# Strided attention pairs in three blocks of residue classes instead of eight, on one core

## The chip, the cores and the metric

The kernel runs on one core of a Trainium2 chip. The metric is the device time in microseconds (us) of one execution; the median of three runs stands for the kernel.

## The reference, cut to what matters

The first part is attention over 8 batches, 8 heads, 576 tokens and a head size of 64. Heads 0 to 3 see a local window; heads 4 to 7 see only earlier tokens of the same residue modulo 32 (the strided heads). The second part is a two-layer network with a squared ReLU on all 4608 tokens.

```python
scores = q @ k.T / 8
mask_local   = (rel >= 0) & (rel < 32)              # rel = query - key; heads 0-3
mask_strided = (rel >= 0) & (key % 32 == query % 32) # heads 4-7
attn = softmax(where(mask, scores, -1e9))
x = (attn @ v)        # tokens x 512, all heads side by side
y = relu(x @ w_in) ** 2 @ w_out                      # 512 -> 2048 -> 512
```

## The kernel before, in words

Work on attention goes by units. A unit is one batch and a pair of heads, numbered u = 4 * batch + pair; pairs 0 and 1 of a batch are local, pairs 2 and 3 strided. The network goes by nine chunks of 512 tokens: `mm1(c, i)` makes one 128-row block of the hidden layer, `mm2(c, i)` a quarter of an output tile. Both run on TensorE (PE) between the attention steps.

A unit goes through these steps. `step_S` multiplies keys with queries into PSUM, and ScalarE (ACT) takes the exponential into a tile `e`. VectorE (DVE) multiplies with a mask (the function `masks`). `step_D` multiplies `e` with V, to which a column of ones is added, so that the sum of each row comes out too; DVE takes the reciprocal of that sum (`rinv`) and multiplies (`x_l` or `x_s`). `step_E` transposes the result into `xt`, the input of `mm1`.

For a strided pair the 576 tokens are sorted by residue modulo 8, because tokens of different residue never meet: eight blocks of 72 tokens for each head. So `step_S` has 16 small matmuls for a pair, `step_D` has 16 in three parts (6, 6 and 4), each part with its own reciprocal and product, and `step_E` has eight PE transposes. Batches 0 and 1 have versions of their own (`step_N`, `step_O`), which the change leaves.

The loads matter here. For a strided pair, q and k are cast to bf16 from DRAM into a DRAM scratch tile by a DMA that GpSimd (POOL) issues (`cast_str_dram`, `q_d` and `k_d`, L165). A transposing DMA issued by SyncE (SP) then brings them into SBUF (`transpose_str`, `qT_s` and `kT_s`, L173). V of batches 2 to 4 is cast straight into its tile `vs` by POOL's DMAs (`load_v_str_direct`, L617). V of batches 5 to 7 comes as fp32 by SP's DMAs into `v_st` (L245), and POOL casts it (L252). Local q and k of batches 5 to 7 are loaded by SP (L114), cast by POOL (L140) and transposed by SP's DMAs (L201).

The order is the program's own. Each engine and each queue runs its instructions in the order in which they were written down, and hooks tie loads and steps to the places between the matmul groups. PE's attention steps are spread over the groups by weights. Three places tie the queues together.

- `load_v_local_gated(b)`, L605: before POOL issues batch b's local V (`vl`), it copies one element of the transposed k of the same batch, so it waits until that has landed. It is used for batches 2 and 3.
- `hold_sync(4)`, L609: SP issues a tiny DMA that reads the last row of batch 4's last V tile, so that SP goes on only when that V has landed. Batch 4's transposes and all of batch 5's loads stand behind it.
- POOL's order for the batches 2 to 5 is: rows (local q and k), casts of q and k, gate, local V, strided V, then rows and casts of the next batch. Casts of batch 5 follow batch 4's V.

In batches 6 and 7 the result of a strided pair is written to DRAM (`x_d`, L446) and transposed back by a DMA (L447); in batches 2 to 5, PE transposes it.

Of the kernel before, what the change touches and what calls it, by code (L numbers as in the profile page):

```python
# [14 lines left out]
def kernel(  # L15
# [21 lines left out]
    NBS = 2 * NJ  # L37
    VP = 72

    singles = ctx.enter_context(tc.tile_pool(name="singles", bufs=1))  # L40
# [32 lines left out]
    mask_full = singles.tile([128, NL, QL], BF16)  # L73
    mask_str = singles.tile([SP_, 1, SP_], BF16)
    vl_all = singles.tile([128, NV, 2, NL, VP], BF16, name="vl")
    vls = [vl_all[:, i] for i in range(NV)]
    vss = [singles.tile([SP_, NBS, VP], BF16, name=f"vs{i}") for i in range(NV)]
    vl_sts = [singles.tile([128, 2 * NL, D], FP32, name=f"vl_st{i}") for i in range(2)]
# [83 lines left out]
    def cast_str_dram(b):  # L162
        for name, src in (("q", q), ("k", k)):
            t = dram.tile([4 * SP_, NJ * D], BF16, name=f"{name}_d")
            nc.gpsimd.dma_start(  # L165
                out=t.rearrange("(x y) c -> x (y c)", x=16),
                in_=src[b, H // 2:H].rearrange("h (x y) d -> (h x) (y d)", x=4))
            big[b, name] = t

    def transpose_str(b):  # L170
        for name in "qk":
            o = strT.tile([128, NJ // 2, 4 * SP_], BF16, name=f"{name}T_s")
            nc.sync.dma_start_transpose(out=o, in_=big.pop((b, name)))  # L173
            came[b] = o[0:1, 0, 0:1]
            for i in range(2):
                st.setdefault(4 * b + 2 + i, {})[name + "T"] = o[:, :, 2 * SP_ * i:2 * SP_ * (i + 1)]

# [47 lines left out]

    def load_v_str_sw(b):
        t = v_st.tile([SP_, 2, NJ * D], FP32, name="v_st")
        t = t.rearrange("p h c -> p (h c)").bitcast(BF16).rearrange("p (h c) -> p h c", h=4)
        nc.gpsimd.dma_start(out=t, in_=v[b, 4:8].rearrange("h (p j) d -> p h (j d)", j=NJ))
        for i in range(2):  # L230
            st.setdefault(4 * b + 2 + i, {})["vf"] = t[:, 2 * i:2 * i + 2]

    def load_v_local_sw(b):
# [5 lines left out]
        for u in range(2):  # L239
            st.setdefault(4 * b + u, {})["v"] = vls[i + u]  # L240

    def load_v_str(u, eng):
        b, p = units[u]
        t = v_st.tile([SP_, 2, NJ * D], FP32, name="v_st")
        eng.dma_start(out=t, in_=v[b, 2 * p:2 * p + 2]  # L245
                      .rearrange("h (p j) d -> p h (j d)", j=NJ))
        st.setdefault(u, {})["vf"] = t

    def cast_v_str(u, copy=None):
        s = st[u]  # L250
        t = vss[v_slot(u)]
        (copy or nc.gpsimd.tensor_copy)(t[:, :, 0:D], s["vf"].rearrange("p h (j d) -> p (h j) d", d=D))  # L252
        s["v"] = t
# [55 lines left out]
    def step_S(u, at_once=False):  # L309
        s = st[u]  # L310
        qT, kT = s["qT"], s["kT"]
        local = is_local(u)
        w, n = (QL, NL) if local else (SP_, NJ)
        kn = 128 if local else SP_
        hn = n // 2
        e = es[u % 4]
        s["e"] = e
        pss = [[None, None], [None, None]]
        for half in range(2):
            for row in range(2):  # L320
                pss[row][half] = bank("pt")
                if u < 4:
                    bias = bias_l[:, half].rearrange("p t c -> p (t c)") if local \
                        else bias_s.rearrange("p t c -> p (t c)")
                    nc.tensor.matmul(pss[row][half][0:kn, 0:S // 2], ident[0:kn, 0:kn], bias,
                                     start=True, stop=False, skip_group_check=True)
            for i in range(hn):
                t = half * hn + i
                klo = w * t
                for row in range(2):  # L330
                    rows = slice(64 * row, 64 * row + 64)
                    if not local:
                        c0 = w * (t // 4)
                        lhsT, rhs = (a[rows, t % 4, c0:c0 + w] for a in (kT, qT))
                    else:
                        lhsT, rhs = kT[rows, klo:klo + kn], qT[rows, w * t:w * (t + 1)]
                    nc.tensor.matmul(pss[row][half][0:kn, w * i:w * (i + 1)], lhsT, rhs,  # L337
                                     start=u > 3, stop=True, skip_group_check=u < 4)
# [11 lines left out]
        def masks(row):  # L350
            x = e[0:kn, S * row:S * (row + 1)].rearrange("p (t c) -> p t c", c=w)
            m = mask_full if local else mask_str.to_broadcast([kn, n, w])
            nc.vector.tensor_tensor(x, x, m, op=ALU.mult)  # L353
# [51 lines left out]
    def step_D(u, part):  # L405
        run_due(lambda x: x[1] == u)
        s = st[u]
        e, vt = s["e"], s["v"]
        if is_local(u):
            w, kn, n0, n1, tot = QL, 128, 6 * part, 6 * part + 6, 2 * NL  # L410
            rhs = vt.rearrange("p h t d -> p (h t) d")
            pos = lambda n: QL * n
            src = lambda n: n
        else:
            w, kn, tot = SP_, SP_, NBS
            n0, n1 = ((0, 6), (6, 12), (12, 16))[part]
            rhs = vt
            pos = lambda n: SP_ * blk_pos(n % 2, n // 2)
            src = lambda n: NJ * (n % 2) + n // 2
        po = bank("ph" if u < 2 else "pt")[:, 0:6 * (D + 1)].rearrange("p (n d) -> p n d", d=D + 1)  # L420
        for n in range(n0, n1):
            nc.tensor.matmul(po[:, n - n0, :], e[0:kn, pos(n):pos(n) + 128],  # L422
                             rhs[0:kn, src(n), 0:D + 1], start=True, stop=True)
        if part == 0:
            s["x"] = (xl_pool if is_local(u) else x_pool).tile(
                [w, tot, D], BF16, name="x_l" if is_local(u) else "x_s")
        x = s["x"]
        if is_local(u):
            x = x.rearrange("p (t h) d -> p h t d", h=2)[:, part]
        else:  # L430
            x = x[:, n0:n1, :]
        m = n1 - n0
        rinv = small.tile([128, 6, 1], FP32, name="rinv")
        nc.vector.reciprocal(rinv[0:w, 0:m], po[0:w, 0:m, D:D + 1])  # L434
        nc.vector.tensor_tensor(x, po[0:w, 0:m, 0:D],  # L435
                                rinv[0:w, 0:m].to_broadcast([w, m, D]), op=ALU.mult)

    def step_E(u):
# [3 lines left out]
        local = is_local(u)  # L442
        n, w = (NL, QL) if local else (NJ, SP_)
        if not local and b >= XD:
            xd = dram.tile([S, 2 * D], BF16, name="x_d")
            nc.sync.dma_start(out=xd.rearrange("(p j) c -> p (j c)", j=NJ), in_=x.rearrange("p n d -> p (n d)"))  # L446
            nc.sync.dma_start_transpose(out=xt[p][:, b * S:(b + 1) * S], in_=xd)  # L447
            st.pop(u)
            return
# [6 lines left out]
        px = bank("pt").bitcast(BF16)[:, 0:S]  # L456
        for t in range(n):
            nc.tensor.transpose(px[:, w * t:w * (t + 1)],  # L458
                                x[:, 2 * t:2 * t + 2, :].rearrange("p h d -> p (h d)"),
                                ident[0:w, 0:w])  # L460
        dst = xt[p][:, b * S:(b + 1) * S]
        copy = nc.scalar.copy if u < 12 else nc.vector.tensor_copy
        if local:
            copy(dst, px)
        else:
            copy(dst.rearrange("c (p j) -> c p j", j=NJ),
                                  px.rearrange("c (j p) -> c p j", j=NJ))
        st.pop(u)
# [100 lines left out]
    def stream_steps(lo, hi, base):  # L569
        order = [T_(lo, "q"), T_(lo, "k"), T_(lo + 1, "q"), S_(lo), T_(lo + 1, "k"), lambda: None]  # L570
        ends = {}
        for u in range(lo, hi + 1):
# [10 lines left out]
            if u < hi:  # L583
                if more:
                    order.append(T_(u + 2, "q"))
                order.append(D_(u, 1))
                if not is_local(u):
                    order.append(D_(u, 2))
        return order, ends
# [18 lines left out]
    def hold_sync(b):  # L608
        nc.sync.dma_start(out=dram.tile([1, 2], BF16, name="hold"),  # L609
                          in_=vss[v_slot(4 * b + 3)][0:1, NBS - 1, 0:2])  # L610

    def load_v_str_direct(b):
        for u in (4 * b + 2, 4 * b + 3):
            t = vss[v_slot(u)]
            h = 2 * units[u][1]
            for i in range(2):
                nc.gpsimd.dma_start(out=t[:, NJ * i:NJ * (i + 1), 0:D],  # L617
                                    in_=v[b, h + i].rearrange("(p j) d -> p j d", j=NJ))
            st.setdefault(u, {})["v"] = t
# [61 lines left out]
    def late_constants():  # L681
# [4 lines left out]
        for t in vss:  # L686
            nc.vector.memset(t[:, :, D:D + 1], 1.0)
        for i, e in enumerate(es):
# [5 lines left out]
    for fn, spare in first:  # L694
        fn()
        warm(spare)
        tick()
    late_constants()
    loads_1()

# [66 lines left out]
    def D_all(u):  # L767
        return [D_(u, i) for i in range(2 if is_local(u) else 3)]

# [14 lines left out]
    second(23, ts("k", 1))  # L784
    second(24, E_(5))
    second(25, S_(6, True))
    second(27, S_(7, True))
# [66 lines left out]
```

## Time and profile before

| | |
|---|---|
| median of 3 runs | 309.14 us (308.31 to 309.71) |
| the profiled execution's own time | 314.03 us |
| its span, first to last instruction | 312.3 us |
| PE busy | 299.8 us (96%) |
| DVE, ACT, POOL busy | 157.9, 167.3, 73.7 us |
| DMA packets, bytes | 94118, 40.75 MB |
| POOL's queue, SP's queue: share of 16 engines | 41.0%, 35.8% |
| mean granted TensorE clock | 0.989 |

A profile is of one execution; this one took 1.6% longer than the median. "L422" is line 422 of the kernel. In the views, PE is the matmuls and PEld their weight loads; SPq and POOLq are the sequencers of these engines. A line of the waits reads: the engine and line that waited, for whom, microseconds in total, times, longest. A line of a timeline reads: start, length, engine, line, operation, output and input, count, and in brackets the idle time before it and who ended it. POOL's time on a DMA line is the time to issue it, not to move the data. The DMA row of the page gives the busy share of the 16 DMA engines in 40 slices of the span, 7.8 us each.

### The profile page before, as it was taken

The page shows a single profiled execution, that of the slowest core. Times are in us where ns is not written, and L with a number is a line of the kernel's source. Part 1 is how long each engine was busy: PE and PEld are TensorE (multiplying, and loading weights), DVE is VectorE, ACT ScalarE, POOL GpSimd, SP SyncE. Part 2 cuts the span into 40 slices and gives each one's busy share as a digit, 9 for nine tenths or more (in the row PEclk, how much of TensorE's full clock was granted, in tenths as well). Part 3 has the DMA queues.
Part 4 walks back from the last instruction along what each step waited for, and adds up shares of the span by engine and source line. Part 5 has one row for each costly group of instructions (what it writes and reads, how often), then busy time and mean ns, then how long its engine had stood idle before and what let it go on. Part 6 is the DMA issues. An engine that isn't in the chain of part 4 may idle for free.

```text
span 312.3 us, 6071 instructions
## 1 busy us (share of the span) xinstructions
PE 299.8 (96%) x2326; PEld 150.9 (48%) x2368; DVE 157.9 (51%) x405; ACT 167.3 (54%) x346; POOL 73.7 (24%) x103
## 2 busy tenths in 40 slices
PE   8799999999999999799999999999999999999995
PEld 3554554544655554344445454444444444444444
DVE  5346764558777865567467668544522222222200
ACT  3666746889567765355545455555443434344311
POOL 8553400630971004434065134000000000000000
PEclk9959999999999999999999999999999999999999
DMA  8999996995999998989899884212221001001121
GB/s 158 177 205 204 191 221 132 177 187 108 154 197 141 100 161 188 198 181 215 141 242 226 213 197 100 73 52 55 71 73 67 35 34 36 34 34 36 48 87 68
DMA packets 94118, 40.75 MB, mean 130 GB/s; under 512 B 78858, under 2 KB 87754, under 8 KB 93898
## 3 DMA queue, kind: packets, MB, share of 16 engines
q0 software_dynamic: 34528, 15.00, 41.0%
q1 hardware_dynamic: 59562, 25.37, 35.8%
q8 instruction: 18, 0.29, 0.4%
q14 instruction: 10, 0.08, 0.1%
HBM read 37.64 MB, written 13.57 MB: 164 GB/s over the span
## 4 chain that ended last, share of the span: by engine, by line
PE 85%; DMA 5%; DVE 4%; POOL 2%; issue 2%; ACT 1%; SPq 0%; POOLq 0%; DVEq 0%
PE ph L482 35%; PE py L522 26%; PE ph L522 9%; PE pt L337 3%; PE pt L422 3%; DMA vl<-in_v_dram 3%; DMA kTl<-k_l 2%; PE pt L482 2%; PE pt L288 1%; PE pt L458 1%; PE ph L504 1%; DMA vl_st<-in_v_dram 1%; PE pt L522 1%; DVE x_l L435 1%; DVE e L353 1%
## 5 line engine op out<-in xcount | busy, mean ns | idle before, releaser
L482 PE MATMUL ph<-xt,w_in_b 128*128 128x512 bf16 x534 | 138.2, 380 | 1.2 <-issue 0.5
L488 ACT ACTIVATE r<-ph 128x512 bf16<-128x512 f32 x138 | 82.3, 597 | 94.1 <-PE ph L482 90.1
L491 DVE TENSOR_TENSOR g_sb<-r 128x512 bf16<-128x512 bf16 x144 | 64.9, 452 | 107.8 <-ACT r L488 106.6
L522 PE MATMUL py<-w_out_b,g_sb 128*128 128x512 bf16 x385 | 100.8, 379 | 0.9 <-issue 0.2
L482 PEld LDWEIGHTS <-w_in_b 128*128 128x128 bf16 x576 | 52.5, 98 | 55.8 <-issue 1.0
L522 PEld LDWEIGHTS <-g_sb 128*128 128x128 bf16 x560 | 50.8, 98 | 54.7 <-issue 0.4
L347 ACT ACTIVATE e<-pt 72x288 bf16<-72x288 f32 (+1 forms) x128 | 45.7, 407 | 12.2 <-PE pt L337 12.2
L522 PE MATMUL ph<-w_out_b,g_sb 128*128 128x512 bf16 x139 | 34.2, 379 | 0.2
L422 PEld LDWEIGHTS <-e 128*128 128x128 bf16 (+1 forms) x384 | 20.5, 98 | 15.9 <-issue 1.7
L435 DVE TENSOR_TENSOR x_s<-pt,rinv 72x384 bf16<-72x384 f32 (+1 forms) x36 | 18.3, 509 | 1.2
L526 ACT COPY y<-py 128x512 f32<-128x512 f32 x25 | 14.6, 585 | 7.0 <-PE py L522 6.3
L353 DVE TENSOR_TENSOR e<-e,mask_str 72x576 bf16<-72x576 bf16 x28 | 14.2, 518 | 3.8 <-ACT e L347 3.7
L435 DVE TENSOR_TENSOR x_l<-pt,rinv 96x384 bf16<-96x384 f32 x28 | 15.5, 554 | 1.0
L434 DVE RECIPROCAL rinv<-pt 96x6 f32<-96x6 f32 (+2 forms) x64 | 11.8, 184 | 6.5 <-PE pt L422 6.3
L353 DVE TENSOR_TENSOR e<-e,mask_full 128x576 bf16<-128x576 bf16 x28 | 12.7, 455 | 1.9 <-ACT e L347 1.7
L220 POOL CAST vl<-vl_st 128x768 bf16<-128x768 f32 x6 | 5.7, 950 | 31.0 <-DMA vl_st<-in_v_dram 30.9
L422 PE MATMUL pt<-vs,e 72*128 72x65 bf16 x192 | 12.1, 194 | 0.7 <-DVE e L353 0.3
L526 ACT COPY y<-ph 128x512 f32<-128x512 f32 x9 | 5.2, 583 | 13.3 <-PE ph L522 13.1
L140 POOL CAST q_l<-q_st 96x768 bf16<-96x768 f32 x6 | 5.2, 866 | 28.0 <-DMA q_st<-in_q_dram 27.9
L617 POOL DMA_DIRECT2D vs<-in_v_dram x12 | 9.7, 817 | 0.0
L422 PE MATMUL pt<-vl,e 128*128 128x65 bf16 x168 | 9.7, 193 | 0.0
L337 PEld LDWEIGHTS <-kT_s 64*72 64x72 bf16 x256 | 6.1, 115 | 7.0 <-issue 6.2
(110 smaller groups left out, 203.6 us busy)
## 6 DMA issues: line engine op xcount, KB each, us to landing
out_dram<-y SPq DMA_DIRECT2D x35, 256.0 KB, 2.3
w_out_b<-in_moe_w_out_dram POOLq DMA_DIRECT2D x4, 512.0 KB, 14.4
q_d<-in_q_dram POOLq DMA_DIRECT2D x6, 288.0 KB, 8.0
k_d<-in_k_dram POOLq DMA_DIRECT2D x6, 288.0 KB, 9.3
q_st<-in_q_dram SPq DMA_DIRECT2D x12, 144.0 KB, 4.1
k_st<-in_k_dram SPq DMA_DIRECT2D x12, 144.0 KB, 4.0
vl_st<-in_v_dram SPq DMA_DIRECT2D x12, 144.0 KB, 3.1
v_st<-in_v_dram SPq DMA_DIRECT2D x6, 288.0 KB
```

The costliest lines, as they stand in the source:

```text
L337: nc.tensor.matmul(pss[row][half][0:kn, w * i:w * (i + 1)], lhsT, rhs, start=u > 3, stop=True, skip_group_check=u < 4)
L347: nc.scalar.activation(e[0:kn, lo:lo + S // 2], pss[row][half][0:kn, 0:S // 2], AF.Exp, scale=scale)
L353: nc.vector.tensor_tensor(x, x, m, op=ALU.mult)
L422: nc.tensor.matmul(po[:, n - n0, :], e[0:kn, pos(n):pos(n) + 128], rhs[0:kn, src(n), 0:D + 1], start=True, stop=True)
L434: nc.vector.reciprocal(rinv[0:w, 0:m], po[0:w, 0:m, D:D + 1])
L435: nc.vector.tensor_tensor(x, po[0:w, 0:m, 0:D], rinv[0:w, 0:m].to_broadcast([w, m, D]), op=ALU.mult)
L482: nc.tensor.matmul(ph, w_in_b[:, kk, 128 * ff:128 * (ff + 1)], xt[kk][:, 512 * c:512 * (c + 1)], start=(kk == order[0]), stop=(kk == order ...
L488: nc.scalar.activation(r, ph, AF.Relu)
L491: later(1, lambda: nc.vector.tensor_tensor(g[:, ff, :], r, r, op=ALU.mult))
L522: nc.tensor.matmul(py, g[:, ff, 128 * j:128 * (j + 1)], w_out_b[:, ff, :], start=(ff == 0), stop=(ff == 15))
L526: nc.scalar.copy(y, py)
L617: nc.gpsimd.dma_start(out=t[:, NJ * i:NJ * (i + 1), 0:D], in_=v[b, h + i].rearrange("(p j) d -> p j d", j=NJ))
```

## The change

For strided units of batches 2 to 7 (u > 7), tokens are sorted by residue modulo 16 and kept in three blocks for each half: three residue classes of 36 tokens make a block of 108, the third block has the remaining two classes (72). q and k lie as rows of two neighbouring tokens (2 x 64 values, 256 B in bf16), so even tokens come to the partitions 0 to 63 and odd ones to 64 to 127; a "row" of `step_S` is now a parity and a "half" a head. A new mask `mask_blk` (108 x 288) fits. V holds two tokens side by side with a one at both ends, so that each parity finds its column of ones.

What the instructions become, for a pair: `step_S` 12 matmuls (108 or 72 columns) for 16, `step_D` 12 matmuls in two parts for 16 in three, `step_E` six PE transposes for eight. A cast of q or k is four DMAs (one a head, 36 x 8 runs of 128 values) for one; a pair's V is six DMAs of 36 rows (three or two runs of 128 values) for two, or for one where SP issues it; `x_d` is six DMAs for one. POOL's cast of V is two instructions for one. `late_constants` follows `loads_1` now and makes the first 108 columns of the mask; two DVE copies at group 24 make the rest. The order of SP's queue stays but for two local transposes of x, which stand one output store later.

```diff
+    PS16 = NA * STRIDE // 16
+    KB = 3 * PS16
+    BLK = ((0, KB), (KB, KB), (2 * KB, S // 2 - 2 * KB))
 def cast_str_dram(b):
-            t = dram.tile([4 * SP_, NJ * D], BF16, name=f"{name}_d")
-            nc.gpsimd.dma_start(
-                out=t.rearrange("(x y) c -> x (y c)", x=16),
-                in_=src[b, H // 2:H].rearrange("h (x y) d -> (h x) (y d)", x=4))
+            t = dram.tile([2 * S, 2 * D], BF16, name=f"{name}_d")
+            tv = t.rearrange("(h j p) c -> h p j c", h=4, j=8)
+            for h in range(4):
+                nc.gpsimd.dma_start(out=tv[h], in_=src[b, 4 + h].rearrange("(p j r) d -> p j (r d)", j=8, r=2))
+    def v_str_pieces(u):
+        b, p = units[u]
+        for h in range(2):
+            vv = v[b, 2 * p + h].rearrange("(p x r) d -> p x (r d)", x=8, r=2)
+            for j in range(3):
+                n = 3 if j < 2 else 2
+                yield slice(PS16 * j, PS16 * (j + 1)), h, slice(0, n), vv[:, j:j + 3 * n - 2:3, :]
 def load_v_str(u, eng):
-        t = v_st.tile([SP_, 2, NJ * D], FP32, name="v_st")
-        eng.dma_start(out=t, in_=v[b, 2 * p:2 * p + 2]
-                      .rearrange("h (p j) d -> p h (j d)", j=NJ))
+        t = v_st.tile([KB, 2, 3, 2 * D], FP32, name="v_st")
+        for rows, h, blks, src in v_str_pieces(u):
+            eng.dma_start(out=t[rows, h, blks], in_=src)
 def load_v_str_direct(b):
-            for i in range(2):
-                nc.gpsimd.dma_start(out=t[:, NJ * i:NJ * (i + 1), 0:D],
-                                    in_=v[b, h + i].rearrange("(p j) d -> p j d", j=NJ))
+            for rows, h, blks, src in v_str_pieces(u):
+                nc.gpsimd.dma_start(out=t[rows, h, blks, V0:V0 + 2 * D], in_=src)
 def step_S(u, at_once=False):
+                    if blocks:
+                        lo, m = BLK[i]
+                        cols = slice(S // 2 * half + lo, S // 2 * half + lo + m)
+                        nc.tensor.matmul(pss[row][half][0:m, lo:lo + m], kT[rows, cols], qT[rows, cols],
+                                         start=True, stop=True)
+                        continue
 def step_D(u, part):
-            n0, n1 = ((0, 6), (6, 12), (12, 16))[part]
+        for n in range(6):
...
+                h, i = n % 2, n // 2
+                lo, kn = BLK[i]
+                pos = S * part + S // 2 * h + lo
+                c0 = V0 + D if part else V0 - 1
+                rhs = vt[0:kn, h, i, c0:c0 + D + 1]
+            nc.tensor.matmul(po[:, n, :], e[0:kn, pos:pos + 128], rhs, start=True, stop=True)
 def step_E(u):
-            nc.sync.dma_start(out=xd.rearrange("(p j) c -> p (j c)", j=NJ), in_=x.rearrange("p n d -> p (n d)"))
+            xv = xd.rearrange("(p j) c -> p j c", j=16)
+            for j in range(3):
+                m = 3 if j < 2 else 2
+                for r in range(2):
+                    nc.sync.dma_start(out=xv[:, 2 * j + r:2 * j + r + 6 * m - 5:6, :],
+                                      in_=x[PS16 * j:PS16 * (j + 1), r, 0:m])
 stream_steps
                 order.append(D_(u, 1))
-                if not is_local(u):
-                    order.append(D_(u, 2))
 hold_sync
-                          in_=vss[v_slot(4 * b + 3)][0:1, NBS - 1, 0:2])
+                          in_=vss[v_slot(4 * b + 3)][KB - 1:KB, 1, 1, V0:V0 + 2])
 late_constants
+        mb = mask_blk[:, 0, :]
...
+        nc.gpsimd.affine_select(out=mb[:, 0:KB], in_=mb[:, 0:KB], compare_op=ALU.is_ge, fill=0.0,
+                                base=0, channel_multiplier=-1, pattern=[[1, KB]])
```

## The prediction

> **What bounds the kernel now.** I read the page's slices and chain first, then what PE waited for between 20 and 200 us, then the two DMA queues (POOL and SP) in order of time, with the landing times that the trace has for each DMA. From the page:
>
> ```profile
> PE 299.8 (96%) x2326; PEld 150.9 (48%) x2368; DVE 157.9 (51%) x405; ACT 167.3 (54%) x346; POOL 73.7 (24%) x103
> ...
> DMA  8999996995999998989899884212221001001121
> ...
> PE 85%; DMA 5%; DVE 4%; POOL 2%; issue 2%; ACT 1%; SPq 0%; POOLq 0%; DVEq 0%
> ```
>
> TensorE sets the end: a 512-column matmul follows the last one every 0.215 us almost throughout. The DMA row is full until slice 24 (190 us), so the loads run only just ahead. How close shows in what PE (here its weight loads) waited for:
>
> ```profile
> PEld L337 <- DMA kTl<-k_l: 2.3, 1, 2.3
> ...
> PEld L337 <- DMA kT_s<-k_d: 0.4, 1, 0.4
> ```
>
> Only two DMA waits after the start-up, both around batches 4 and 5: the strided S(18) at 115.4 us and the local S(20), which stood from 129.7 to 132.08. Both come late for one reason, seen in SP's and POOL's waits and SP's timeline:
>
> ```profile
> SPq L609 <- DMA vs<-in_v_dram: 11.7, 1, 11.7
> ...
> 108.49 0.30 SPq L609 DMA_DIRECT2D hold<-vs  x1
> 108.90 2.73 SPq L173 DMA_TRANSPOSE qT_s<-q_d  x1
> 111.73 1.30 SPq L173 DMA_TRANSPOSE kT_s<-k_d  x1
> ...
> 124.48 0.91 SPq L245 DMA_DIRECT2D v_st<-in_v_dram  x2
> 125.48 1.20 SPq L201 DMA_TRANSPOSE qT<-q_l  x1
> 126.78 1.22 SPq L201 DMA_TRANSPOSE kTl<-k_l  x1
> ```
>
> SP stands until the last V of batch 4 has landed (108.48). Behind `hold` are queued batch 4's transposes, all loads of batch 5, and its transposes: 6.6 us after it kT_s of batch 4 lands (115.05), 23.6 us after it kTl of batch 5 (132.04). There is no slack. What sets 108.48 is POOL's queue:
>
> ```profile
> POOL vl L605 <- DMA kT_s<-k_d: 30.6, 2, 18.7
> POOL w_in_b L257 <- DMA vl<-in_v_dram: 2.0, 1, 2.0
> ...
> 59.33 3.24 POOL L617 DMA_DIRECT2D vs<-in_v_dram  x4
> ...
> 77.01 0.28 POOL L605 COPY vl<-kT_s 1x1 bf16<-1x1 bf16 x1 [11.94 <-DMA kT_s<-k_d]
> ```
>
> L605 holds each batch's V until its kT_s is there, so the batches form a chain: casts, transpose, gate, V, next casts. The L257 line is a limit on depth: the program gives a queue's DMAs eight semaphores in turn, and an issue waits for the DMA eight before it (w_in_b went out at 13.81, after vl, eight issues earlier, landed at 13.52).
>
> **What the skill says.** "DMA: Bandwidth & Descriptors", Anatomy of one DMA: about 2.0 us per DMA are fixed, mostly completion. The trace agrees roughly: q_d on a quiet queue at 134.59 landed after 4.06 us, of which its packets took 1.4 and the issue 0.5. Same page, Rules for kernel authors: merge small transfers, under 64 KB they are mostly overhead. The new V DMAs write 18 or 27 KB; no run yet shows such a size from POOL. Same page, the section on why a DMA increments its semaphore by 16: the engines used are the largest number up to 16 that divides the slowest dimension, so 12 of 16 for 36 rows, as for 72; the trace does not show it.
>
> **The change, part by part.**
>
> *PE.* Consecutive L422 weight loads of 72 rows start 29 ns apart. D falls from 16 to 12 matmuls: 4 x 0.029 = 0.12 us a unit. S falls from 16 to 12, in pairs, with the same 576 columns per row group: about 0.03. PE transposes: same columns, nothing. Twelve units: 1.8 us. The half before S(20) only makes PE wait longer, so 0.9 counts.
>
> *DVE.* A third reciprocal (174 ns) and product go: per unit 3 x 187 + 2 x 553 + 421 against 2 x (187 + 553), about 0.6 us. PE waited on DVE under 2 us in 20 to 200 us, so I count nothing; Exp (L347: 402 ns on 72 rows, 412 on 128) and the mask (518 against 455 for the 128-row one) stay. The new mask, memsets and copies are about 1.2 us of DVE behind matmuls; POOL's one select (0.3) falls where POOL waits for DVE anyway (33.95). If those covers fail, 1 us.
>
> *POOL issues.* V of a batch: 12 DMAs for 4; q and k: 8 for 2. A DMA of this shape costs 0.69 us with 288 runs (L153), 0.81 with 576 (L617), 1.2 with 2304 (L237): I take 0.64 for 108 runs and 0.70 for 288. V: 7.7 for 3.2 us; casts: 5.6 for 1.1. So +9 us of POOL per batch, in a queue with gates.
>
> *Packets.* Today a cast is 16 packets of 18432 B at 1376 to 1568 ns, landing 1.4 us after its predecessor. As 256 B rows it is 1152. The queue's 128 B packets take 38 ns each, 768 B ones 85, hence some 47 for 256 B; in the densest 4 us 128 B packets passed at 15.5 ns, and the 400 GB/s read at that time by long ones would give 25. Per DMA of 288 rows, 24 to an engine: 0.6 to 1.1 us, I take 0.75. So q and k take 6 us for 2.8. V's packets halve (1152 of 128 B a unit become 576), a relief of up to 2 us a batch. Transposes: 1152 packets as before.
>
> *The chain, with these.* Batch 2: its casts now wait for semaphores of the w_out loads (46.14, 47.21, 48.66) and land at 54.7 for 51.43; kT_s at 58.3 for 56.66 (+1.7). Gate 58.5; vl lands 64.8 and 65.9 (needed 68.59). Vs: six out by 64.8, the seventh and eighth wait for vl, the last leaves at 69.2 (62.6). Rows of batch 3 until 70.6, casts until 76.2, last landing 80.5 (73.26), kT_s about 84 (76.96): **+7**. V of batch 3, gated, lands at 91.0 for 83.85; PE wants it for D(12) at 87.2: **a new stall of 3.8**. Then rows 88, vs with waits for vl and rows until 97, casts until 102.7, memsets 104, vl 106 (landing 110.5, D(16) now needs it at 113), vs until 113.8, landing 116.5: **`hold` +8**. kT_s of batch 4 lands at 123, PE would be at 119.2: a further 3.9.
>
> *SP.* v_st of batches 5 to 7: 12 issues for 2, at 0.38 to 0.5 each some 5.4 us for 0.9, the later ones waiting for the landing eight before. Today kTl behind them is held by v_st's own data (landed 130.9, kTl 132.04) rather than by its issue, so I take +3.5 of the 4.5 to 6. kTl for S(20): 132.04 + 8 + 3.5 = 143.5: **+11.5**, the two stalls before it included. Batches 6 and 7 have slack (kTl landed 153.1 for 163.9, 177.6 for 189.7), enough for 5 us. x_d: 6 issues for 1, +1.8 us and perhaps a longer landing than 2.0; its readers come 14 groups (about 12 us) later: nothing; cover gone, 2 us.
>
> Sum: +11.5 - 0.9 = **+10.6**. The profiled execution took 314.03 (span 312.3 and 1.7 around it), 1.6% over the median of 309.14; the sum makes 324.6 of its own time and 319.7 of the median. A measurement tells about 0.5% (1.5 us) from no change.
>
> Bounds of the unknown. Issue cost of a 108-run DMA: 0.5 (the cheapest here, 16 runs) to 0.8. With 0.5, a landing after 2.5 us and light casts, kT_s of batch 3 is 2 late, D(12) doesn't stall, `hold` is 2 late, SP adds 2 to 3: net +3 to +4, less for a lucky order. With 1.1 us a cast DMA, `hold` is 12 late and SP adds 6: +17. Writing 256 B rows to DRAM is not shown in the trace; were it twice a packet's price, the casts reach that end.
>
> **Rivals.**
> *Not slower (decided on the other side).* The place is `hold`. Today its V took 16 us from issue to landing, so DMA, not POOL's issue, may set it, and V's packets halve. If POOL's extra issues only eat this backlog and the v_st issues hide behind v_st's data, the gain stays: 309.1 - 1.8 = 307.3, at best -4 if S(20)'s wait goes too. It decides from the point where `hold` comes no later than 108.5. For it: landings of 12 to 17 us there. Against: in batches 2 and 3 they were 5 to 9 us, and kT_s gates V without any backlog (POOL stood 11.9 us at L605).
> *SP alone.* POOL hides, v_st does not: +3.5 - 0.9, about 311.7.
> *Casts clog.* DRAM rows of 256 B run at the high price, and x_l's transposes mix with them as at 91 to 107 (landing after 10 to 14 us instead of 2.5): about 326.
> *The change not doing what it says* is excluded for counts by the program's order; only sizes are open.
>
> **Numbers.** Main chain 0.63 (its own range 314 to 324), casts clog 0.17, SP alone 0.12 (0.02 of it within 0.5%), not slower 0.08 (half faster, half within 0.5%). Hence slower 0.90, same 0.06, faster 0.04. The range, 311 to 328, takes in the light and the heavy bound and leaves out mainly the not-slower case.
>
> **What would show it.** Right: POOL issues of a batch's V lasting 8 us and more; waits of vs on vl's landing; PE waiting at the first local D of batch 3 and at S(18), S(20) for `kT_s` and `kTl`; `hold` near 116; SP's v_st block of 5 us; D's matmuls 144 for 192 at an unchanged 29 ns. Wrong: `hold` before 110, or no PE gap over 1 us between 80 and 145. If `hold` is late but the end is not, PE had slack that I missed.

## The result, and the profile after

The changed kernel takes **325.77 us** (median of four runs, 325.20 to 329.90) against 309.14: a ratio of 1.0569, 95% interval 1.0479 to 1.0659. It is slower by 16.6 us; the prediction said 10.6. The profiled execution of the changed kernel took 325.71 us of its own time (span 324.0), so here the profile stands for the median. That of the kernel before did not: its TensorE clock was at half from 16.2 to 23.0 us. Most of its executions don't have that (71 of 78 later ones have a mean clock of 0.998 or more). I therefore profiled the kernel before once more, and where a number below is "before", it is from that second profile (own time 309.21, span 307.5) unless the text says "first profile". S(18) is `step_S` of unit 18, D(12) is `step_D` of unit 12. A ratio compares means, and leaves out executions over 1.5% above the fastest of their kernel, so it need not be the quotient of the medians.

The page of the changed kernel, the lines that answer to those shown of before (busy time by engine, the granted clock and the DMA share in 40 slices of 8.1 us, the last chain by engine, the groups of POOL's DMA issues):

```profile
PE 303.7 (94%) x2256; PEld 149.6 (46%) x2256; DVE 148.8 (46%) x389; ACT 167.5 (52%) x346; POOL 112.9 (35%) x170
...
PEclk9999999999979996999999999999999999999999
DMA  8999999979999999889975999534131011001021
...
PE 57%; DMA 22%; POOL 12%; issue 5%; SPq 2%; ACT 1%; DVE 1%; POOLq 0%; DVEq 0%
...
L637 POOL DMA_DIRECT2D vs<-in_v_dram x36 | 22.6, 635 | 4.1 <-DMA vl<-in_v_dram 1.6
...
L172 POOL DMA_DIRECT2D k_d<-in_k_dram x24 | 15.7, 658 | 4.6 <-DMA w_out_b<-in_moe_w_out_dram 1.8
L172 POOL DMA_DIRECT2D q_d<-in_q_dram x24 | 15.8, 664 | 2.7 <-DMA w_out_b<-in_moe_w_out_dram 2.2
```

PE's share of the last chain is 57% for the first profile's 85%, DMA's 22% for 5%, POOL's 12% for 2%. POOL is busy some 40 us longer, nearly all of it issuing: 36 V DMAs at 635 ns (22.6 us, for 9.8) and 48 casts at some 660 ns (31.5, for 12 casts in 6.3). The clock row has two dents, slices 12 and 16 (89 to 97 and 121 to 130 us). What PE waited for between 40 and 240 us (engine, line, releaser: microseconds in total, times, longest):

```profile
PE pt L342 <- DMA kT_s<-k_d: 5.6, 1, 5.6
PE pt L436 <- DMA vl<-in_v_dram: 3.7, 2, 3.0
PE ph L545 <- ACT r L511: 2.1, 1, 2.1
PE ph L505 <- DMA xt<-x_l: 1.8, 2, 1.6
```

The first is S(18), strided batch 4; the second is D(12), local batch 3. The same view of before, for PE, has no wait over 0.4 us in this window. The last chain, in order of time (start, length, what), shows where PE's waits come from:

```profile
63.89 2.37 POOL vs L637 x4
...
69.00 2.62 POOL q_d L172 x4
71.62 1.95 POOL k_d L172 x3
...
82.37 0.19 POOL vl L626
...
85.53 7.89 DMA k_st<-in_k_dram
...
93.71 3.20 POOL vs L637 x5
96.92 2.62 POOL q_d L172 x4
...
105.46 3.59 POOL vs L637 x6
...
110.83 2.48 POOL vs L637 x4
...
116.84 7.51 DMA kT_s<-k_d
124.39 0.76 PE pt L342 x12
```

From 58 to 124 us the end is set by POOL's queue: V of batch 2, casts of batch 3, gate (L626), V of batch 3, casts of batch 4, V of batch 4, and then the transpose behind `hold` that S(18) needs. The 7.9 us of `k_st` is the rows' DMA of batch 4, for which a V DMA eight issues later had to wait. SP's timeline has that end of it and what follows (start, length, line, output and input, count):

```profile
114.69 0.30 SPq L630 DMA_DIRECT2D hold<-vs  x1
...
116.84 2.06 SPq L178 DMA_TRANSPOSE kT_s<-k_d  x1
...
132.09 5.83 SPq L251 DMA_DIRECT2D v_st<-in_v_dram  x12
...
139.37 1.21 SPq L206 DMA_TRANSPOSE kTl<-k_l  x1
```

In before, POOL's gate of batch 3 and SP's queue were earlier:

```profile
75.96 0.29 POOL L605 COPY vl<-kT_s 1x1 bf16<-1x1 bf16 x1 [11.36 <-DMA kT_s<-k_d]
...
103.28 0.30 SPq L609 DMA_DIRECT2D hold<-vs  x1
...
118.71 0.96 SPq L245 DMA_DIRECT2D v_st<-in_v_dram  x2
```

`hold` moved by less than POOL's issues did. The last V of batch 4 was issued at 92.5 us in before and landed 10.8 us later; in the changed kernel it was issued at 112.7 and landed after 2.0. So of the 20.2 us by which it is issued later, the quicker landing gives back 8.8, and 11.4 reach `hold`. Behind `hold`, kTl of batch 5 landed 27.2 us later, for 23.2 in before: at 141.9 for 126.5.

Where the time went is read from the start of the S steps of both profiles:

| step | before, us | after, us | difference | what lies between |
|---|---|---|---|---|
| S(8) | 59.7 | 60.3 | +0.6 | |
| S(11) | 72.6 | 75.4 | +2.8 | PE waits 2.1 for a PSUM bank (ACT) |
| S(14) | 86.7 | 93.9 | +7.2 | D(12) waits 3.0 and 0.7 for `vl`; clock at half for 3.4 |
| S(17) | 105.1 | 111.6 | +6.5 | |
| S(18) | 112.3 | 124.4 | +12.1 | S(18) waits for `kT_s` |
| S(19) | 119.2 | 135.1 | +15.9 | clock at half for 6.8 |
| S(20) | 127.1 | 142.9 | +15.8 | |
| S(31) | 204.9 | 223.5 | +18.6 | PE waits for `xt`, 1.6 at 156 and 0.4 at 223 |
| end | 307.5 | 324.0 | +16.5 | |

The changed order of steps puts four network matmuls (0.9 us) more ahead of S(19) and S(20), and eight ahead of S(31). With these taken off, 15.0 of the 16.5 us are lost by S(20); the waits for `xt` add 2.0 after it, and 0.5 is won back by the end.

### The profile page after: what moved, and what is told of

It reads as the page before. It is cut to its first block, busy times and chain, and to the rows that moved or that the text cites. A ratio compares the mean times of both kernels' runs of the same rounds, so it can differ in the third digit from the quotient of the medians.

```text
span 324.0 us, 6032 instructions
## 1 busy us (share of the span) xinstructions
PE 303.7 (94%) x2256; PEld 149.6 (46%) x2256; DVE 148.8 (46%) x389; ACT 167.5 (52%) x346; POOL 112.9 (35%) x170
## 4 chain that ended last, share of the span: by engine, by line
PE 57%; DMA 22%; POOL 12%; issue 5%; SPq 2%; ACT 1%; DVE 1%; POOLq 0%; DVEq 0%
PE py L545 23%; PE ph L505 23%; DMA vl<-in_v_dram 7%; PE ph L545 5%; POOL vs L637 4%; DMA xt<-x_l 3%; DMA kT_s<-k_d 3%; DMA w_in_b<-in_moe_w_in_dram 3%; DMA k_st<-in_k_dram 2%; POOL q_d L172 2%; PE pt L436 2%; POOL k_d L172 1%; DMA x_d<-x_s 1%; POOL vl L235 1%; PE ph L527 1%
## 5 line engine op out<-in xcount | busy, mean ns | idle before, releaser
L505 PE MATMUL ph<-xt,w_in_b 128*128 128x512 bf16 x552 | 141.1, 381 | 2.5 <-DMA xt<-x_l 1.8
L511 ACT ACTIVATE r<-ph 128x512 bf16<-128x512 f32 x138 | 82.3, 597 | 97.8 <-PE ph L505 96.6
L545 PE MATMUL py<-w_out_b,g_sb 128*128 128x512 bf16 x400 | 104.5, 384 | 0.0
L360 ACT ACTIVATE e<-pt 128x288 bf16<-128x288 f32 (+2 forms) x128 | 45.8, 410 | 15.8 <-PE pt L350 8.1
L637 POOL DMA_DIRECT2D vs<-in_v_dram x36 | 22.6, 635 | 4.1 <-DMA vl<-in_v_dram 1.6
L172 POOL DMA_DIRECT2D k_d<-in_k_dram x24 | 15.7, 658 | 4.6 <-DMA w_out_b<-in_moe_w_out_dram 1.8
L172 POOL DMA_DIRECT2D q_d<-in_q_dram x24 | 15.8, 664 | 2.7 <-DMA w_out_b<-in_moe_w_out_dram 2.2
L446 DVE RECIPROCAL rinv<-pt 96x6 f32<-96x6 f32 (+1 forms) x52 | 9.8, 189 | 12.1 <-PE pt L436 12.0
L436 PE MATMUL pt<-vl,e 128*128 128x65 bf16 x168 | 10.5, 199 | 4.1 <-DMA vl<-in_v_dram 4.1
L447 DVE TENSOR_TENSOR x_s<-pt,rinv 108x384 bf16<-108x384 f32 x24 | 13.4, 558 | 0.8
L342 PE MATMUL pt<-qT_s,kT_s 64*108 64x108 bf16 x144 | 6.3, 220 | 5.6 <-DMA kT_s<-k_d 5.6
L367 DVE TENSOR_TENSOR e<-e,mask_blk 108x576 bf16<-108x576 bf16 x24 | 11.1, 481 | 0.7 <-ACT e L360 0.7
```

The lines of the kernel that those rows point to most:

```text
L172: nc.gpsimd.dma_start(out=tv[h], in_=src[b, 4 + h].rearrange("(p j r) d -> p j (r d)", j=8, r=2))
L360: nc.scalar.activation(e[0:kn, lo:lo + S // 2], pss[row][half][0:kn, 0:S // 2], AF.Exp, scale=scale)
L436: nc.tensor.matmul(po[:, n, :], e[0:kn, pos:pos + 128], rhs, start=True, stop=True)
L446: nc.vector.reciprocal(rinv[0:w], po[0:w, :, dc:dc + 1])
L447: nc.vector.tensor_tensor(x, po[0:w, :, x0:x0 + D], rinv[0:w].to_broadcast([w, 6, D]), op=ALU.mult)
L505: nc.tensor.matmul(ph, w_in_b[:, kk, 128 * ff:128 * (ff + 1)], xt[kk][:, 512 * c:512 * (c + 1)], start=(kk == order[0]), stop=(kk == order ...
```

## The experiments

Medians in us; the ratio is to the kernel before in the same series (308.6 to 308.9), with its 95% interval. "Gate" is the copy that POOL makes when kT_s of batch 3 has landed (L626 in the changed kernel). Gate, `hold` and waits are of the profiled execution.

| kernel | median | ratio | gate | `hold` | PE's waits at D(12), S(18), S(20) |
|---|---|---|---|---|---|
| before, once more | 309.21 | one run | 76.0 | 103.3 | 0.4, 0, 0 |
| after | 325.77 | 1.0569 | 82.4 | 114.7 | 3.7, 5.6, 0 |
| 1 before, rows of 256 B | 310.57 | 1.0061 [1.0041, 1.0081] | 78.8 | 104.4 | 1.3, 0, 0 |
| 2 before, also four casts | 311.93 | 1.0104 [1.0072, 1.0136] | 76.8 | 103.8 | 0, 0, 0 |
| 3 before, V in six DMAs a pair | 318.96 | 1.0338 [1.0306, 1.0370] | 81.0 | 111.9 | 0, 2.4, 2.7 |
| 4 after, few V, few casts | 311.67 | 1.0034 [1.0003, 1.0066] | | | not read, see there |
| 5 the same, zeros later | 308.79 | 1.0009 [0.9990, 1.0027] | 75.7 | 98.9 | 0.8, 0, 0 |
| 6 after, few casts | 320.30 | 1.0342 [1.0267, 1.0417] | 80.5 | 117.0 | 4.0, 5.9, 1.3 (in an execution of 324.4) |
| 7 after, few V | 310.40 | 1.0057 [1.0029, 1.0085] | 76.6 | 104.3 | 0, 0, 0 |
| 8 after, few V on POOL only | 312.38 | 1.0116 [1.0078, 1.0154] | 75.8 | 101.5 | 0, 0, 2.3 |
| 9 after, no `hold` | 321.73 | 1.0402 [1.0343, 1.0462] | 83.4 | none | 3.4, 0, 4.2 |
| 10 after, other order | 319.51 | 1.0358 [1.0315, 1.0401] | 76.5 | 112.4 | 1.9, 0, 6.4 |
| 11 after, PE kept busy | 326.88 | 1.0605 [1.0559, 1.0651] | 83.1 | 116.0 | 3.8, filled, 2.2 |

**The kernel before, once more.** No edit.

> The kernel before, unchanged, for a profile whose own time lies near its median; the profile shown before was 4.9 us over it. Queue theory (too many small DMAs in POOL's and SP's queues, passed on by the gate of batch 3 and by hold): about 309 us, S(8) some 3 us earlier than the 63.3 us of the first profile, hold again at 105 to 109 us, a wait for kTl before S(20). If the first profile's wait before S(20) was a part of its own slowness, PE has no DMA wait over 1 us here.

Its own time was 309.21, its clock 0.998, and PE had no DMA wait over 0.4 us from 40 us on. `hold` came at 103.28, not 108.49, and S(20) began at 127.1 without the 2.35 us wait of the first profile. So the expectation's last sentence holds, and the first profile showed a tighter kernel than the usual one. With the half clock at 16 to 23 us PE came 3.6 us later to S(8), 63.3 against 59.7. But POOL issued the last V of batch 4 at nearly the same time, 92.8 and 92.5; it landed 5.2 us later. Whether the half clock is the cause of that is not shown: experiment 2's profile has it too, from 15.9 to 22.8 us, and `hold` at 103.8.

**1 and 2: packets against DMAs.** The kernel before writes q and k as rows of 256 B, in one DMA for each name (1) or in four (2):

```diff
-            t = dram.tile([4 * SP_, NJ * D], BF16, name=f"{name}_d")
+            t = dram.tile([2 * S, 2 * D], BF16, name=f"{name}_d")
             nc.gpsimd.dma_start(
-                out=t.rearrange("(x y) c -> x (y c)", x=16),
-                in_=src[b, H // 2:H].rearrange("h (x y) d -> (h x) (y d)", x=4))
+                out=t.rearrange("(a n) c -> n a c", a=4),
+                in_=src[b, H // 2:H].rearrange("h (p j) d -> (h p) (j d)", j=NJ).rearrange("n (a c) -> n a c", a=4))
# 2: the same for each head h of 4, out=tv[h], in_=src[b, H // 2 + h]...
```

> The kernel before with q and k cast to DRAM in rows of 256 B, still one DMA for each (the transposes read the same number of rows of 256 B). Queue theory: the number of DMAs is what costs, so 309 to 311 us (ratio 1.00 to 1.007). Packet theory (small rows to DRAM and their packets are what costs): at least half of the 16.6 us, 317 us or more.

> As b_rows256, but each cast in four DMAs, one a head: eight for a batch instead of two. Queue theory: POOL issues 4 us more for each batch, and the gate passes that on, 4 to 8 us over b_rows256 (313 to 318 us). Packet theory: the same time as b_rows256 within 1.5 us.

Rows of 256 B cost 1.7 us with their gate 2.9 us later; the four DMAs for one, 48 casts instead of 12, add only 1.4 us more. Kernel 2 missed its 313 to 318, and is within the 1.5 us that the packet theory gave this step; but kernel 1 is far from that theory's 317. While V is few, POOL stands at the gate for 6.8 us in kernel 2 (11.4 in before), and the casts' issue eats of that. So the packets' price is not what costs 16 us.

**3: V alone.** The kernel before, with the V of each strided pair in six DMAs of 24 rows, on POOL and on SP (`hold` reads the last row):

```diff
-        eng.dma_start(out=t, in_=v[b, 2 * p:2 * p + 2].rearrange("h (p j) d -> p h (j d)", j=NJ))
...
+            for x in range(0, SP_, 24):
+                eng.dma_start(out=t[x:x + 24, i], in_=vv[x:x + 24])
...
-                nc.gpsimd.dma_start(out=t[:, NJ * i:NJ * (i + 1), 0:D], in_=v[b, h + i]...)
+                for x in range(0, SP_, 24):
+                    nc.gpsimd.dma_start(out=t[x:x + 24, NJ * i:NJ * (i + 1), 0:D], in_=vv[x:x + 24])
```

> The kernel before with a strided pair's V in six DMAs of 24 rows, from POOL for batches 2 to 4 and from SP for 5 to 7, with runs and bytes as before; hold reads the last row. Queue theory: 4 us more of POOL for each batch and 4 us of SP for batch 5, so 6 to 12 us over before (315 to 321 us), with a wait at the first local D of batch 3 or at S(18). Packet theory: no change, 309 us.

10.1 us without any other part of the change: 36 POOL issues of 614 ns, gate 5.1 us later than before, `hold` 8.6 us later, waits for `kT_s` and `kTl`, and 3.1 us for ACT at 71 us (2.1 in the changed kernel). V's DMA count carries most of the loss, and neither the blocks nor their shapes are needed for it.

**4 and 5: all parts but the counts.** The changed kernel with V in 96-row DMAs (as many as before) and q and k in long rows, one DMA for each. The values of q, k and V then stand in other places than the reference needs; PE, DVE and ACT do the same work as in the changed kernel.

```diff
-            for rows, h, blks, src in v_str_pieces(u):
-                nc.gpsimd.dma_start(out=t[rows, h, blks, V0:V0 + 2 * D], in_=src)
+            for h in range(2):
+                nc.gpsimd.dma_start(out=t[0:96, h, :, V0:V0 + 2 * D],
+                                    in_=v[b, h0 + h].rearrange("(p i r) d -> p i (r d)", i=3, r=2))
+            nc.vector.memset(t[96:KB], 0.0)     # 4: among the late constants; 5: at group 24
... (v_st, the casts and hold to match)
```

> The changed kernel with the number of DMAs of before for q, k and V: each cast in one DMA in the long rows of before, each strided V in as many DMAs as before (96 rows). The values of q, k and V then stand in other places than the attention needs; all work and bytes stay. Queue theory: the gain of PE alone is left, 306 to 310 us. Block theory (the larger blocks, masks, or the shorter steps themselves cost): 316 us or more.

> a_few again (the changed kernel with the number of DMAs of before for q, k and V, their values in other places), with the zeros for the 12 rows of V that are not loaded written at group 24 instead of among the late constants, where they held PE for 2.2 us. Queue theory: no DMA wait is left, and the gain of the blocks shows: 306 to 308.5 us, 1 to 3 us under before. Block theory: 309 us or more.

Both came out above their ranges. In 4, PE waited 2.2 us at about 32 us for the extra zeros (and its profiled execution, 318.5 us, is 2% above its median, so its waits aren't read); so 5 places the zeros later. The result, 308.79 against 308.62, is the kernel before: the blocks themselves cost nothing. PE is busy 298.8 us for 300.6 in before, just the 1.8 us that the prediction had worked out, and the profiled span is 1.5 us shorter (306.0 for 307.5), but the medians do not show it: the interval is 0.9990 to 1.0027. Where the gain goes was not found.

**6 and 7: one count at a time.** In the changed kernel, casts as before (6: the `cast_str_dram` of before in full) or V as in 4 (7, with the zeros among the late constants, so with that 2.2 us wait).

> The changed kernel with each cast of q and k in one DMA in the long rows of before (their values in other places); V as in the change. Queue theory: V's part stays, 314 to 321 us, hold 3 us or more earlier than 114.7. Packet theory: the casts' rows were the cost, 311 us or less.

> The changed kernel with V in as many DMAs as before, of 96 rows (its values in other places); q and k as in the change. Queue theory: the casts' part stays, 312 to 319 us. Packet theory: 321 us or more.

With few V the casts' 48 DMAs cost at most 1.6 us (312 to 319 was expected), and part of that can be the wait for the zeros, which is the experiment's own; the gate is at 76.6, `hold` at 104.3, and PE has no wait at D(12), S(18) or S(20). With few casts, V's DMAs still cost 11.5 us (10.5 if the execution of 324.4 us is left out). That is experiment 3's answer from the other side. But the two don't add up to 17: casts that are nearly free alone are worth 5.5 us (6.5) beside V's DMAs (325.8 for 320.3). The two share POOL's queue, and its slack, 11.4 us at the gate in before, can be used once. POOL's timeline of 7, around batch 3's casts and gate, where it still stands idle (in brackets) for 6.8 us:

```profile
69.13 0.66 POOL L172 DMA_DIRECT2D k_d<-in_k_dram  x1 [0.40 <-DMA k_st<-in_k_dram]
76.60 0.46 POOL L619 COPY vl<-kT_s 1x1 bf16<-1x1 bf16 x1 [6.81 <-DMA kT_s<-k_d]
```

and the same place of the changed kernel, where V of batch 2 stands ahead:

```profile
59.48 3.78 POOL L637 DMA_DIRECT2D vs<-in_v_dram  x6
63.89 3.73 POOL L637 DMA_DIRECT2D vs<-in_v_dram  x6 [0.63 <-DMA vl<-in_v_dram]
...
73.75 0.66 POOL L172 DMA_DIRECT2D k_d<-in_k_dram  x1 [0.19 <-issue]
82.37 0.18 POOL L626 COPY vl<-kT_s 1x1 bf16<-1x1 bf16 x1 [7.96 <-DMA kT_s<-k_d]
```

The idle time at the gate is no slack any more: from the last cast issued at 74.4 to kT_s at 82.3 it is the landing and the transpose. What counts is mainly when the last cast leaves: at 69.8 or at 74.4.

Experiment 6 missed in one point: `hold` came at 117.0, later than in the changed kernel. Its profiled execution, 324.4 us, is 1.3% above its median; in it the clock was at half from 86.9 to 93.7 us, around D(12)'s wait, PE came later to the D steps of batch 3, and six V DMAs waited for PE:

```profile
111.89 3.69 POOL L637 DMA_DIRECT2D vs<-in_v_dram  x6 [4.16 <-PE pt L350]
```

Once PE is late, POOL's queue is late for that reason too: in this execution part of `hold`'s delay is PE's own, come back. Whether executions near the median have it is not on record. How the 5.5 us are made up was not separated further.

**8: POOL's V or SP's V.** V few on POOL (as in 4), twelve `v_st` DMAs on SP and 48 casts kept.

> The changed kernel with V of batches 2 to 4 alone (POOL's) in as many DMAs as before, of 96 rows, values in other places; V of batches 5 to 7 stays at twelve DMAs a batch on SP, q and k at eight casts. POOL theory (SP's twelve issues are hidden; all of the loss comes from POOL's queue before S(19)): 307 to 311 us. SP theory (the prediction's 3.5 us of v_st on the path to S(20)): 312 us or more, with a wait for kTl at S(20).

This is 3.6 us above experiment 5, so the SP theory has it, narrowly. SP's timeline of this kernel:

```profile
117.73 6.86 SPq L251 DMA_DIRECT2D v_st<-in_v_dram  x12
...
126.04 1.21 SPq L206 DMA_TRANSPOSE kTl<-k_l  x1
```

and of experiment 5:

```profile
114.18 1.00 SPq L243 DMA_DIRECT2D v_st<-in_v_dram  x2
...
116.60 1.22 SPq L206 DMA_TRANSPOSE kTl<-k_l  x1
```

The block is 5.9 us longer, and S(20) waits 2.3 us (2.8 by its weight loads) for the `kTl` behind it. SP's share is at most 3.6 us (medians; 3.3 by the profiled spans, 309.3 and 306.0), but the casts are in it. Against experiment 7, which has the casts too, it is 2.0, and 7 has the zeros' wait. So SP's share lies between 2.0 and 3.6 us; the rest of V's 10 to 11.5 us is POOL's.

**9: without `hold`.**

```diff
-    second(64, lambda: hold_sync(4))
```

> The changed kernel without the tiny DMA hold, so that SP need not wait for batch 4's V. Queue theory: the transposes of batch 4 start as soon as their casts have landed (102 to 106 us), the wait of 6.1 us at S(18) goes, and batch 5 is loaded earlier: 315 to 320 us. If the data in the DMA engines were the limit, the loads would only trade places: 324 us or more.

4 us are won; 315 to 320 us was expected. S(18)'s wait goes, and S(20) waits 4.2 us for `kTl` in its place: the transposes of batch 4 are early, but batch 5's loads still run through the same queues. D(12)'s wait of 3.4, which lies ahead of `hold`, stays.

**10: casts ahead of V.** The rows and casts of batch 3 leave before V of batch 2, and `hold` stands behind batch 4's transposes:

```diff
-    second(29, lambda: load_v_local_gated(2), lambda: load_v_str_direct(2), rows(3), lambda: cast_str_dram(3))
+    second(29, lambda: load_v_local_gated(2), rows(3), lambda: cast_str_dram(3), lambda: load_v_str_direct(2))
...
+    plan(4, 64, 61)
     second(64, lambda: hold_sync(4))
-    plan(4, 64, 61)
```

> The changed kernel, complete, with two moves and no DMA less: in POOL's queue batch 2's strided V goes out after the rows and casts of batch 3 instead of ahead of them, and on SP hold stands behind batch 4's transposes instead of ahead. Queue theory: the rows of batch 3 land some 5 us earlier (no wait of ACT at 72 us), gate 3 opens at 75 to 78 us instead of 82.4, the wait at the first local D of batch 3 goes, and S(18) hardly waits; a wait of 2 to 5 us at S(20) may take its place: 313 to 319 us. If POOL's order is not what matters: 323 us or more.

The gate is back at 76.5, D(12)'s wait is halved, ACT's and S(18)'s are gone; S(20)'s grows to 6.4, since `hold` at 112.4 still stands ahead of batch 5. The time is 0.5 us over its range: D(12)'s wait should have gone, and S(20)'s is longer than the 2 to 5 us expected. It wins 6 us of the 17, and is 3.6% slower than before. No version with the change's DMA counts that was run beats the kernel before.

**11: is the half clock a cost of its own?** 28 matmuls on zeros fill PE's wait at S(18):

```diff
+                if u == 18 and half == 0 and row == 0:
+                    pw = bank("ph")
+                    for _ in range(28):
+                        nc.tensor.matmul(pw, idle[:, 0:128], idle, start=True, stop=True)
```

> The changed kernel with 28 matmuls of 512 columns on zeros ahead of S(18), as long as PE's wait there (6.0 us). Clock theory (after a wait of that length PE runs at half clock for 3.4 or 6.8 us, which costs half of that again): the wait stays but the half clock after it goes, 321 to 324 us. If the half clock does not come from PE's idle time: 325 us or more, the same half clock at 124 to 131 us.

The clock theory got its mechanism and not its gain. Windows of the changed kernel (us from the start, length, PE busy and count, the same for PEld, DVE, ACT and POOL, granted clock, DMA share, GB/s):

```profile
118.00:124.40 6.40, 0.85 (x6) 0.21 (x4) 1.10 (x4) 0.60 (x1) 0.51 (x1) 0.95 1.46 176
124.40:135.00 10.60, 10.60 (x56) 4.79 (x56) 3.52 (x9) 3.69 (x8) 4.07 (x5) 0.71 1.24 210
```

and with PE kept busy:

```profile
118.00:124.40 6.40, 6.40 (x36) 3.02 (x35) 2.00 (x6) 1.20 (x2) 1.60 (x3) 1.00 1.61 175
124.40:135.00 10.60, 10.60 (x81) 5.06 (x79) 4.24 (x10) 4.72 (x11) 3.60 (x4) 1.00 1.30 190
```

At full clock S(18) to S(19) takes 7.8 us instead of 10.7, and then S(20) waits 2.2 us for `kTl` and starts at 143.9 (142.9; `hold` came 1.3 us later in this execution). In the changed kernel kTl had landed at 141.9, 1.0 us ahead of S(20), which therefore did not wait: PE, slowed by the half clock, and SP's queue came there almost together. So the half clock after S(18) is real, but at most that 1.0 us of it lies on the path. (The fill ended 1.2 us after kT_s had landed here, which S(20)'s wait covers.) The half clock after D(12) was not tested alone.

## Why the prediction was right, and where its size was off

- **The mechanism: right.** Issues on POOL lie on the chain of 60 us, D(12), S(18) and S(20) come late in that order, and V alone (3) or with few casts (6) is slower by 10 us and more. Two things make POOL late, its issues and its waits for the DMA eight before (3.8 us of waits between 63 and 94 us); no experiment parts them.
- **The issue price: right.** 0.64 and 0.70 us taken, 0.635 and 0.66 measured. The chain's instants: kT_s of batch 3 landed at 82.3 (about 84 forecast), its `vl` at 90.0 (91.0), vs out until 96.9 (97), casts until 102.1 (102.7), `hold` 114.7 (116.5), kT_s of batch 4 at 124.4 (123). D(12)'s stall was 3.7 (3.8).
- **The packets' price: a little high.** Packets of 256 B of these casts took 44 ns on the mean (47 taken), and batch 3's casts landed 0.5 to 0.6 us apart (0.75 taken). The lower bound of 25 ns should be some 20, for 512 B read by one of 16 engines at 400 GB/s; it carries nothing.
- **S(18): under-sized, with little effect.** Its wait was 5.6 for 3.9: kT_s landed 1.4 us later than forecast.
- **SP's block: right.** 5.83 us for 5.4. On the path 3.5 were taken; the way from `hold` to kTl grew by 4.0 (27.2 for 23.2), and experiment 8 gives 2.0 to 3.6.
- **S(20): its instant right, its reason in part luck.** It started at 142.9 for 143.5. But the forecast, and its list of signs, have PE wait there for kTl. kTl landed at 141.9 and PE did not wait; the half clock, which the prediction did not have, brought PE there 1.0 us later. At full clock (11) the wait is there, 2.2 us.
- **The profile's own time: near, 325.71 for 324.6,** and this too is in part luck: the base was an execution 4.9 us over the median.
- **The step that failed: "the sum makes 324.6 of its own time and 319.7 of the median".** The sum's base was S(20) at 132.04, after its own wait, in a profile of 314.03; its result was a place in time at which the queues let S(20) go, not a shift. POOL's gates hardly move with PE (batch 2's opened at 56.79 in the first profile and at 56.37 in the second, while PE's S(8) differed by 3.6), and the issue of batch 4's last V hardly either (92.8, 92.5). What made `hold` and kTl late in the first profile was the slower landing of that V, and in the changed kernel that landing takes only 2.0 us. A usual execution of before reaches S(20) at 127.1 without any wait, so the same forecast of 143.5 costs 16.4 there and not 11.5: with the 0.9 taken off, 324.7. The measured +15.8 at S(20) is that. So 11.5 was the mis-sized term, and 15.8 is what the runs show in its place (0.9 of it is the four matmuls that now stand ahead). The prediction had even noted that the execution stood 1.6% over the median, and let the difference pass to the median unchanged. The main chain's own range, 314 to 324, ends below 325.77; the stated range holds it because it also takes in the heavier cases, up to 328.
- **Not foreseen, small.** ACT stood 2.55 us for the rows of batch 3, which now wait behind twelve V DMAs, and held PE's PSUM bank (ACT's timeline, below). The clock was at half after the waits. PE waited for `xt`, 1.6 us at 156 and 0.4 at 223, which the prediction counted as nothing (for `x_d`) or did not name (for `x_l`).

```profile
72.04 0.83 ACT L145 COPY q_l<-q_st 96x768 bf16<-96x768 bf16 x1 [2.55 <-DMA q_st<-in_q_dram]
```

- **The rivals.** "Casts clog, about 326" has the measured number and not the cause: casts landed 5.0 to 5.4 us after issue (median), rows of 256 B cost 0.6% (1), and the casts' DMAs alone at most 1.6 us (7). "SP alone" was a part of the sum, 2.0 to 3.6 us. "Not slower" falls with 3; its claim that POOL's issues eat only backlog holds for the casts alone (2, 7), and for V in part: the landing of batch 4's last V gave back 8.8 of 20.2 us. Its PE gain of 1.8 us of busy time is there (5).

## What to carry to other kernels

Where a queue of one engine's DMAs has gates in it, count the DMAs and multiply by the issue time, whatever their bytes, and look for how much of it the landing gives back. In experiment 3, twelve V DMAs of a batch for four on POOL (0.614 us each) and for two on SP cost 10 us, while the layout that they served in the changed kernel cost nothing (5). When a change makes the loads later than the compute, its cost is the instant at which the loads let the compute go, less the instant at which a usual execution gets there; take the second from a profile whose time is the median's, or correct for it. Two changes that share a queue's slack have to be tried together: the casts were nearly free alone (1.6 us) and dear beside V's DMAs (5.5).

## What was not expected of the hardware

PE's granted clock fell to 0.5 after waits, for 3.4 or 6.8 us. Taking a wait as the time between the starts of two weight loads: each of 3.46 us or more, up to 7.0, brought it in the runs above (after 6.1 in the changed kernel for 6.8 us, after 4.75 in experiment 9 for 3.4); waits of 2.4 (11) and 2.9 (8) did, and others of 2.3 (the changed kernel), 2.8, 2.9 (11), 3.0 and 3.3 (3) did not. The Trainium skill, "TensorE: Matmul & The Clock Gate", What's actually happening, says that the clock is halved after an idle window of some 3.4 us, and that the window runs freely. The lengths, one or two windows, agree, and so does the free run: in each profile all changes of the clock lie a whole number of 3.413 us apart (in the changed kernel at 4.28, 89.62, 93.03, 123.75 and 130.58 us).

But here a window need not be wholly idle. These changes give the grid of windows, and in each one can add up the time in which no matmul ran, by the profile's modelled ends. Over all 14 profiles, the twelve full-clock windows with 2.10 us or more of it were each followed by the half clock; of the others between 23 us and the last matmul, all with 1.97 or less, none was. So it matters where a wait falls. Experiment 3's of 3.3 us lay across an edge, with 1.7 us of idle time in one window and 1.0 in the next; experiment 11's of 2.4 us lay in one, with 2.2.

The start is another matter: in four profiles, the first of before among them, the half clock came at about 16 us after a window with only 0.6 to 1.0 us without a matmul. What brings it there was not found. In the first profile of before it moved what a reader takes for the kernel's usual slack: in the second it is missing, and S(8) starts 3.6 us sooner.
